# Zero products in 64x32 tiles ahead of the first chain of an attention kernel, and fewer zero products inside it

## Chip, cores and metric

The kernel runs on one core of one Trainium2 chip. The metric is the time of one execution on the device, in microseconds (us); the kernel before takes 241.3 us, the median of three runs (241.25 to 241.42). The profile is of one such execution; its span, first to last instruction, is 239.6 us.

## The reference

An attention with 32 memory slots per head, and behind it a bilinear feed-forward layer. Sizes: 8 batches, 8 heads, 576 positions, head width 64; model width 512, inner width 1536.

```python
def _attn_ref(q, k, v, phi):                 # q, k, v: (8, 8, 576, 64); phi: (8, 8, 576, 32)
    a = softmax(phi over its 32 slots)
    k_m = np.einsum('bhsm,bhsd->bhmd', a, k)
    v_m = np.einsum('bhsm,bhsd->bhmd', a, v)
    scores = 1 / np.sqrt(64) * np.matmul(q, k_m.transpose(0, 1, 3, 2))
    attn = softmax(scores over the slots)
    return np.matmul(attn, v_m)

def _moe_ref(x, w_a, w_b, w_out):            # x: the attention's output, (4608, 512)
    return (x @ w_a * (x @ w_b)) @ w_out
```

## The kernel before

Every instruction is placed by hand: each engine takes its instructions in the order in which the program names them. Batches are handled one after the other in "chains" of short named units. In the first chain, that of batch 0, TensorE has little to do between waits, and the kernel puts products of zeros there ("fill"). Their results are never read.

```python
    warm = consts.tile([P, 512], F16, name="warm")
    nc.vector.memset(warm, 0.0)
    # ... [cut]
    def fill(n, cols=512):
        pw = banks.tile([P, 512], F32, name="pw")
        for _ in range(n):
            nc.tensor.matmul(pw[:, :cols], warm[:, :P], warm[:, :cols], start=True, stop=True)
```

The units of a chain that the reader meets below (b is the batch, g the half of its heads):

```python
        def exp_phi(z):                       # exp0, exp1: ScalarE
            nc.scalar.activation(out=t["exp"][...], in_=phis[b][...], func=AF.Exp)

        def sums(g, x):                       # ks (x = 0) and vs (x = 1): 36 products in 64x32 tiles each
            pk = banks.tile([P, 2 - x, D], F32, name="pk")
            for i in range(NI):               # NI = 9
                for j in range(4):
                    r, hp = head(g, j)
                    nc.tensor.matmul(pk[32 * j:32 * j + 32],
                                     t["exp"][64 * r:64 * r + 64, hp, i, :],
                                     kvs[b][64 * r:64 * r + 64, part, hp, D * i:D * (i + 1)],
                                     start=(i == 0), stop=(i == NI - 1), tile_position=(64 * r, 32 * j))
            # ... [cut] VectorE: kvm = pk times the reciprocal of the softmax's sum

        def transpose(g, x):                  # kt, vt: TensorE transposes kvm, VectorE copies it to kvT
            ...

        def q_transpose(hp):                  # qt0 to qt3: VectorE
            nc.vector.transpose(out=t["qT"][:, hp, :].bitcast(F32), in_=qs[b][:, hp, :].bitcast(F32))

        def scores(gs):                       # s0, s1: 16 products in 32x32 tiles each
            ...

        def exp_scores(g):                    # e0, e1: ScalarE, E = exp(scores)
            ...

        def denominators(g, hfs):             # den00 ...: one product of 128x128 for each half, ScalarE takes its Ln
            for hf in hfs:
                nc.tensor.matmul(pD, ones, t["E"][:, g, sl], start=True, stop=True)
                nc.scalar.activation(out=t["L", g][:, sl], in_=pD, func=AF.Ln)

        def normalise(g, hfs):                # nr00 ...: ScalarE R = exp(-L), VectorE A = E times R
            ...
    # hv, v: "fold", kvT times the weights (pva); hx, x: its copies to vab; a, b: "up" products (pa, pb) of vab and A
```

The program of the chains names them in order. `f18` is `fill(18, 128)`, `L` asks for the loads of a later batch, and `y3` in chain 1 takes three products of the output layer (po).

```python
    def chain(b, plan):
        for x in plan.split():
            if x[0] == "f":
                fill(int(x[1:]), P)
            # ... [cut]
            else:
                us[b][x]()

    fill(64, P)
    chain(0, "exp0 exp1 f18 ks0 ks1 f4 kt0 qt0 qt1 f2 kt1 f4 qt2 qt3 f2 s0 e0 f2 den00 s1 e1 f8 den10 nr00 nr10 vs0 vs1 ...")
    chain(1, "exp0 y3 exp1 y8 ks0 y1 qt0 y2 kt0 y2 qt1 s0 ks1 y3 e0 y1 kt1 qt2 y1 qt3 den0 y3 s1 ...")
```

The loads are asked for by GpSimd in this order: phi, q, v of batch 0 (k comes by two other queues), the weights w_a and w_b in four parts, the output weights and phi, k, q, v of batch 1. Up to eight are under way at a time.

The softmax here doesn't subtract the row's maximum and nothing guards it: scores larger than these inputs give would overflow.

## Time and profile before

| what | before |
|---|---|
| time, median of three | 241.3 us |
| span of the profile | 239.6 us |
| TensorE with a product in flight | 230.6 us (96%) |
| zero products (pw) | 114 of 3092 |
| first and last start of one | 1.3 and 18.3 us |
| DMA traffic from 8 to 30 us | about 205 GB/s |
| share of TensorE in the chain that ended last | 77% |
| share of DMA in it | 16% |

PE is TensorE's products, PEld its weight loads (one for each product), DVE VectorE, ACT ScalarE, POOL GpSimd. Products overlap: a row's first start and its length until the last end say more than the busy time. "Idle before <- X" is the time in which the engine had nothing under way and what ended it; "issue" means that it waited for nothing that the profile shows. The chain that ended last is followed back from the last instruction, at each step to what released it.

### The profile page before, as it was taken

How to read it: one execution, taken by the hardware profiler on the slowest of the kernel's cores; microseconds unless marked ns; L12 is line 12 of the kernel's file. 1: busy time of each engine (PE TensorE's matmuls, PEld its weight loads, DVE VectorE, ACT ScalarE, POOL GpSimd, SP SyncE). 2: the span in 40 equal slices, each digit the busy share in tenths (PEclk: the TensorE clock that was granted, in tenths of full speed). 3: DMA queues.
4: the chain of work that ended last, by engine and by line, in shares of the span. 5: the costliest groups of instructions: out<-in, count | busy, mean ns of one | idle time of the engine just before them, and what ended most of it. 6: DMA issues, size and time to landing. Idle time of an engine off the chain costs nothing.

```text
span 239.6 us, 7764 instructions
## 1 busy us (share of the span) xinstructions
PE 230.6 (96%) x3092; PEld 170.3 (71%) x3092; DVE 165.4 (69%) x403; ACT 158.7 (66%) x410; POOL 159.5 (67%) x135
## 2 busy tenths in 40 slices
PE   7958999999999999999999999999999999999993
PEld 7734664456757867878787787878787778888882
DVE  4636784469949878966975659775976585756642
ACT  2266671669698599687776867797776877465330
POOL 7953244499979629981799948984769087937001
PEclk9999999999999999999999999999999999999998
DMA  6999999999967954992359945599130303032155
GB/s 230 239 197 207 206 258 206 252 213 279 224 154 161 214 115 98 222 208 49 43 123 233 211 90 65 141 212 191 41 85 11 81 16 74 10 83 61 38 130 125
DMA packets 28164, 34.71 MB, mean 145 GB/s; under 512 B 4416, under 2 KB 22208, under 8 KB 28128
## 3 DMA queue, kind: packets, MB, share of 16 engines
q0 software_dynamic: 19264, 23.14, 52.2%
q1 hardware_dynamic: 8352, 10.29, 18.4%
q10 hardware_dynamic: 512, 0.79, 1.0%
q8 instruction: 24, 0.39, 0.7%
q14 instruction: 12, 0.10, 0.1%
HBM read 42.47 MB, written 9.44 MB: 217 GB/s over the span
## 4 chain that ended last, share of the span: by engine, by line
PE 77%; DMA 16%; DVE 2%; issue 1%; POOL 1%; ACT 1%; DVEq 0%; POOLq 0%
PE py L473 18%; PE pa L601 18%; PE pb L601 17%; PE pv L473 9%; DMA wb_sb<-in_moe_w_b_dram 6%; DMA q_sb<-in_q_dram 5%; PE pva L343 5%; DMA kv_sb<-in_v_dram 4%; PE px L473 4%; PE po L398 2%; PE pkv L212 2%; PE pscore L297 1%; PE pD L320 1%; DVE ht L612 1%; ACT a_sb L609 1%
## 5 line engine op out<-in xcount | busy, mean ns | idle before, releaser
L612 DVE TENSOR_TENSOR ht<-a_sb,pb 128x288 f16<-128x288 f16 x168 | 73.3, 450 | 37.5 <-ACT a_sb L609 26.8
L601 PEld LDWEIGHTS <-vab 128*128 128x128 f16 x768 | 72.4, 98 | 24.9 <-issue 7.8
L609 ACT CAST a_sb<-pa 128x288 f16<-128x288 f32 x168 | 66.7, 407 | 25.7 <-PE pa L601 24.6
L601 PE MATMUL pa<-A,vab 128*128 128x288 f16 x384 | 75.8, 287 | 0.1
L601 PE MATMUL pb<-A,vab 128*128 128x288 f16 x384 | 75.0, 286 | 0.7 <-ACT vab L355 0.5
L455 POOL TENSOR_TENSOR h_sums<-ht 128x768 f16<-128x768 f16 x28 | 46.0, 1644 | 33.9 <-DVE ht L612 33.7
L473 PEld LDWEIGHTS <-h_sums 128*128 128x128 f16 x384 | 37.0, 98 | 7.7 <-issue 1.1
L355 DVE CAST vab<-pva 128x512 f16<-128x512 f32 (+1 forms) x52 | 32.3, 644 | 4.8 <-PE pva L343 4.2
L355 ACT CAST vab<-pva 128x512 f16<-128x512 f32 (+1 forms) x52 | 27.7, 569 | 7.8 <-PE pva L343 7.2
L473 PEld LDWEIGHTS <-ht 128*128 128x128 f16 x288 | 28.1, 98 | 5.7 <-issue 0.4
L473 PE MATMUL py<-w_sums,h_sums 128*128 128x256 f16 x192 | 31.3, 273 | 0.0
L455 POOL TENSOR_TENSOR h_sums<-h_sums,ht 128x768 f16<-128x768 f16 x14 | 23.0, 1640 | 1.0
L455 POOL TENSOR_TENSOR h_sums<-ht,h_sums 128x768 f16<-128x768 f16 x14 | 23.0, 1642 | 0.9
L310 ACT ACTIVATE E<-pscore 128x288 f16<-128x288 f32 x32 | 11.4, 419 | 11.4 <-PE pscore L297 11.2
L331 POOL TENSOR_TENSOR A<-E,R 128x576 f16<-128x576 f16 x12 | 15.3, 1278 | 4.3 <-ACT R L329 4.3
L473 PE MATMUL py<-wo_sb,ht 128*128 128x256 f16 x96 | 16.7, 273 | 0.0
L473 PE MATMUL pv<-w_sums,h_sums 128*128 128x256 f16 x96 | 16.5, 273 | 0.0
L473 PE MATMUL py<-w_sums,ht 128*128 128x256 f16 x96 | 15.9, 272 | 0.1
L473 PE MATMUL px<-wo_sb,ht 128*128 128x256 f16 x96 | 15.9, 273 | 0.0
L321 ACT ACTIVATE L<-pD 128x288 f32<-128x288 f32 x32 | 11.5, 418 | 6.0 <-PE pD L320 5.8
L480 ACT ACTIVATE u<-py 128x256 f32<-128x256 f32 x32 | 12.5, 390 | 4.3 <-PE py L473 3.7
L203 DVE STREAM_TRANSPOSE qT<-q_sb 128x288 f32<-128x288 f32 x32 | 14.6, 464 | 0.3 <-DMA q_sb<-in_q_dram 0.3
(65 smaller groups left out, 275.7 us busy)
## 6 DMA issues: line engine op xcount, KB each, us to landing
out_dram<-o_sb SPq DMA_DIRECT2D x68, 128.0 KB, 2.4
phi_sb<-in_phi_dram POOLq DMA_DIRECT2D x8, 576.0 KB, 5.4
kv_sb<-in_v_dram POOLq DMA_DIRECT2D x7, 576.0 KB, 10.3
kv_sb<-in_k_dram POOLq DMA_DIRECT2D x7, 576.0 KB, 6.6
q_sb<-in_q_dram POOLq DMA_DIRECT2D x6, 576.0 KB, 13.1
wo_sb<-in_moe_w_out_dram POOLq DMA_DIRECT2D x6, 256.0 KB, 13.7
q_sb<-in_q_dram POOLq DMA_DIRECT2D x4, 288.0 KB, 9.7
wa_sb<-in_moe_w_a_dram POOLq DMA_DIRECT2D x2, 512.0 KB, 13.8
```

Of the source, the lines that this page charges most:

```text
L203: nc.vector.transpose(out=t["qT"][:, hp, :].bitcast(F32), in_=qs[b][:, hp, :].bitcast(F32))
L310: nc.scalar.activation(out=Ev[:, g, :, z, :], in_=pss, func=AF.Exp, scale=1.0 / (8.0 * CS))
L321: nc.scalar.activation(out=t["L", g][:, sl], in_=pD, func=AF.Ln)
L331: engine.tensor_tensor(out=attn[b][:, g, sl], in0=t["E"][:, g, sl], in1=t["R", g][:, sl], op=ALU.mult)
L343: nc.tensor.matmul(t["pva", lo, z][g][0][32 * j:32 * j + 32, 0:hi - lo], t["kvT"][64 * r:64 * r + 64, 4 + g, M * j:M * j + M], w_sbs[z][64 ...
L355: engine_copy(out=vabs[b][z][:, g, lo:hi], in_=pva[:, 0:hi - lo])
L455: engine.tensor_tensor(out=out, in0=in0, in1=in1, op=op)
L473: nc.tensor.matmul(po, lhs[:, i], rhs[:, i], start=first and i == 0, stop=i == KH - 1, skip_group_check=not first)
L480: nc.scalar.mul(out=x, in_=po, mul=scale)
L601: nc.tensor.matmul(ps, vabs[b][x][:, g, P * i:P * (i + 1)], attn[b][:, g, HALF * hf:HALF * (hf + 1)], start=(g == 0), stop=(g == 1))
L609: nc.scalar.copy(out=a_sbs[b, i, hf], in_=ps)
L612: nc.vector.tensor_tensor(out=ht[:, i, t0:t0 + HALF], in0=a_sbs.pop((b, i, hf)), in1=ps, op=ALU.mult)
```

## The change

A second helper issues zero products in tiles of 64 rows and 32 columns, 64 columns of zeros each, four column positions in turn. 48 of them stand ahead of the first chain between two groups of the products of before: 46, 48 in tiles, 14, in place of 64. Within the chain the group ahead of the first sums goes from 18 to 8 and the one ahead of the first scores from 4 to 2; the groups of 2 ahead of s0 and of den00 and the group of 8 ahead of den10 go; a group of 4 comes in ahead of vs0. In all there are 138 zero products instead of 114, and fewer of them stand between the chain's own units. It serves to keep TensorE supplied with activity ahead of the chain while standing less in the way inside it. What is computed stays the same.

```diff
+    def fill_tiles(n):
+
+        pw = banks.tile([P, 64], F32, name="pw")
+        for x in range(n):
+            j = x % 4
+            nc.tensor.matmul(pw[32 * j:32 * j + 32], warm[0:64, 0:32], warm[0:64, 0:64],
+                             start=True, stop=True, tile_position=(0, 32 * j))
 ...
-    fill(64, P)
-    chain(0, "exp0 exp1 f18 ks0 ks1 f4 kt0 qt0 qt1 f2 kt1 f4 qt2 qt3 f2 s0 e0 f2 den00 s1 e1 f8 den10 nr00 nr10 vs0 vs1 den01 den11 nr01 f4 vt0 vt1 hv0a nr11 hx0a f6 a0.0 ... [the rest as before]")
+    fill(46, P)
+    fill_tiles(48)
+    fill(14, P)
+    chain(0, "exp0 exp1 f8 ks0 ks1 f4 kt0 qt0 qt1 f2 kt1 f2 qt2 qt3 s0 e0 den00 s1 e1 den10 nr00 nr10 f4 vs0 vs1 den01 den11 nr01 f4 vt0 vt1 hv0a nr11 hx0a f6 a0.0 ... [the rest as before]")
```

## The prediction

> **What bounds the kernel now.** I read the page first. TensorE has something in flight nearly all the time, at full granted clock, so zero products can only cost or save where TensorE waits.

> ```profile
> PE 230.6 (96%) x3092; PEld 170.3 (71%) x3092; DVE 165.4 (69%) x403; ACT 158.7 (66%) x410; POOL 159.5 (67%) x135
> ...
> q8 instruction: 24, 0.39, 0.7%
> ```

> The second line matters more than it looks. TensorE ran 3092 products and as many weight loads, 6184 instructions; 24 packets are 258 instructions each, and 0.39 MB over 6184 is 63 bytes. So I read queue 8 as TensorE's own program, arriving during the run in packets of 256 instructions, 128 products.

> Then the timeline of TensorE in the stage that the change touches (start, duration, what, products, and the idle time before them):

> ```profile
> 13.19 0.51 PE L151 MATMUL pw<-warm 128*128 128x128 f16 x6
> 14.71 0.27 PE L151 MATMUL pw<-warm 128*128 128x128 f16 x2 [1.01 <-issue]
> 14.82 0.28 PE L320 MATMUL pD<-E,ones 128*128 128x288 f16 x1
> 15.03 0.78 PE L260 MATMUL pk<-kv_sb,exp_sb 64*32 64x64 f16 x72
> ```

> A zero product waits for no data, yet one group of eight (f8) breaks in two: from the last start at 13.48 to the next at 14.71 are 1.23 us. The rows of the timeline before it add up to 82+72+4+8+2+8+6+16+2+1+16+6 = 223 products and one more weight load. Counting on, the same happens exactly 128 products later, and again after 5x128 more:

> ```profile
> 20.68 1.22 PEld L601 LDWEIGHTS <-vab 128*128 128x128 f16 x11 [0.33 <-issue]
> ...
> 65.87 0.09 PEld L297 LDWEIGHTS <-kvT 32*32 32x32 f16 x1 [0.17 <-issue]
> ```

> In the record of DMA packets the three packets concerned start at 12.29, 18.48 and 63.55 us, and TensorE goes on 2.42, 2.19 and 2.32 us later. So I take these three as waits for instructions: about 1.15 us at 14.7, 0.35 at 20.7, 0.2 at 65.9. Where DMA traffic is light late in the run, packets start when TensorE is some 185 instructions into a block of 256. I therefore place the request at 120 to 170 instructions of each block (an estimate). The first falls at 7.1 to 8.1 us, so under the full load of that time it waited 4 to 5 us.

> Last, the chain of waits in order of time, for the window up to 46 us:

> ```profile
> 3.70 10.74 DMA kv_sb<-in_v_dram
> ...
> 14.72 15.07 DMA wb_sb<-in_moe_w_b_dram
> ...
> 30.08 11.94 DMA q_sb<-in_q_dram
> 42.02 0.02 issue
> 42.04 0.85 DVE qT L203 x2
> ...
> 42.94 0.44 PE pscore L297 x14
> ```

> Up to 42 us it holds no TensorE work. The input loads run back to back at about 205 GB/s, and the scores of batch 1 wait for the last of q. What TensorE gains before 42 us is waiting time there, unless a load also gets faster.

> [...] the zero products start 106.7 ns apart until 6.2 us, 55.7 ns after. [...] 72 tile products of 64 columns take 0.59 us from first start to last (8.2 ns each), and a change of mode costs about 0.2 us between starts (14.82 to 15.03). [...]

> **The change part by part.** *Ahead of the chain.* Before: 82 zero products (64 and f18), 1.26 to 8.19 us; the first sums then start at 8.41, released by ScalarE's exp of phi. After: 46 x 106.7 ns = 4.91 us, to 6.17; a change of mode, 0.2; 48 tile products x 8.2 ns = 0.4; a change back, 0.2; 14+8 = 22 x 55.7 ns = 1.2 us. That ends at 8.2 us. So nothing moves here, but 116 products have passed instead of 82, and the first request for instructions (product 60 to 85) falls into the tiles, at 6.2 to 6.6 instead of 7.1 to 8.1 us: some 1.2 us earlier.

> *Inside.* The groups f4, f2, f2 and f8 become f2, none, none and none; 14 products go. Those around the first scores cost nothing, because the scores wait for the transposed q (DVE until 11.32). f8 is 0.45 us of zero products, 0.33 of them ahead of the stall and inside the 1.01. The new f4 ahead of the v sums costs 0.2 us.

> *Where the first stall goes.* After 223.5 products the program again runs dry. Now 116+72+4+8+2+8+2 = 212 lie ahead of the first scores, so it runs dry at their twelfth of 16 products, at about 11.5 us instead of 13.5. The packet: request at 6.4, wait 3.5 to 5, then 2.3 to 2.4 to TensorE's next product gives 12.3 to 13.8, about 12.9. From there by the durations of before: rest of the scores and exp of E 1.1 us, first denominator, scores of the second half 0.35, their exp until 2.55 us after the stall's end. There the denominator den10 starts: 15.45 against 14.82. From den10 run Ln, two exps and two multiplies to the scaled v (kvm, 16.47, 1.65 us after den10), on which the v transposes and the rest of batch 0 wait. So batch 0 is about 0.6 us late (0 to 1.5).

> *The second stall.* After 24 more products in all, the boundary lies 48 instructions earlier in the work, at the first "up" product (18.6 us, 19.2 with the delay). Its request comes before the first stall now (10.7 against 12.8 us), plus the 8.0 us that the second took gives 18.7. It no longer stalls: minus 0.4 us. Net at 36 us: about 0.2 late. The wait for q at 42 us (vector engine idle 0.26, TensorE 0.42) takes that up.

> *After 42 us.* TensorE is the bound: gaps over 0.12 us between starts add up to only 2.2 us. The seventh stall had 7.6 us from request to boundary and needed 7.3 to 7.6; shifted by 48 instructions it has 9.0, so 0.2 us go. The fifth has 6.75 instead of 8.2 where it needed 6.7, so a small stall could appear.

> Sum: 241.3 + 0.6 - 0.4 - (0.2, hidden by the wait for q) - 0.15 = about 241.2 us.

> **The rivals.** *The stall disappears.* If the early request meets a still short queue and is served within 2.7 us, den10 starts at 14.05 and batch 0 gains up to 0.7 us. For it: the early packets of phi go at 400 GB/s, twice the later rate. Against it: the next two packets waited over 4 us too. Even then the loads of k (landed 36.6, just when TensorE was ready) and q hide the gain: 241.0.

> *The stall in the scores is worse than the one it replaces.* There it delays a chain of exp, denominator, scores and exp, while before two of these had passed. With the packet at 13.8, batch 0 is 1.5 late, 1.1 after the second stall's gain, 0.8 after q's slack: 242.0.

> *The clock.* If tile products do not count as activity or fewer zero products let the clock fall, the 22 products ahead and the first sums run at half rate: about 1.2 us more at 8.2 and perhaps 241.8. Against it: 0.4 us of tiles behind 4.9 us of full products is little, and the page shows full clock through the gap of 1.2 us.

> *A load changes.* Each instruction packet holds one DMA engine for about 0.95 us; of v's shares, 15 had landed by 13.2 us and the last at 14.4. The packets come sooner but not more often before 42 us, so q should land at 42.0 again.

> **Range and chances.** All outcomes lie within 1 us of 241.3, because the change moves waits of about 1 us in front of a load that ends at 42 us whatever TensorE does. I take 241.2, with 240.7 to 242.0 for the uncertain packet. Two per cent would be 4.8 us; nothing here reaches it: 1% faster, 98% within, 1% slower.

> **What would show it.** In the profile after: the sums of batch 0 start at 8.4 us again; the group of eight is gone, and an "issue" gap of 1 to 2 us stands inside the first scores at 11.5 to 13; the first instruction packet starts at 10 to 11.5; no gap at the second boundary near 19; q of batch 1 lands at 42.0 within 0.3; scores of batch 1 near 42.9. It is wrong if the scores of batch 0 run without a gap, if the request is not tied to the count of instructions, or if q lands over 0.5 us away from 42.0.

## The result, and the profile after

The changed kernel takes 257.76 us (median of four runs, 257.09 to 258.16) against 241.28 us (241.16 to 241.42) for the kernel before: a ratio of 1.068 [1.0656, 1.0704]. It is 6.8% slower, far outside the predicted 240.7 to 242.0. The page of its profile (first the busy time of TensorE, then the granted clock in 40 slices, queue 8 and one group of products) shows where to look:

```profile
PE 232.8 (91%) x3116; PEld 170.4 (67%) x3116; DVE 178.7 (70%) x403; ACT 159.1 (62%) x410; POOL 159.3 (62%) x135
...
PEclk9977999965799999999999999999999999999999
...
q8 instruction: 24, 0.39, 0.7%
...
L609 PE MATMUL pa<-A,vab 128*128 128x288 f16 x384 | 77.7, 293 | 13.0 <-DVE vab L363 13.0
```

Three things are new. VectorE is busy for 13.3 us more with the same 403 instructions. One "up" product pa waits 13.0 us for VectorE's vab. The clock has two dips, at about 15 to 22 and 53 to 66 us. Queue 8 still brings 24 packets.

**Batch 0 runs partly at half clock.** The timeline of TensorE after (start, duration, what, products, idle before):

```profile
8.44 1.26 PE L268 MATMUL pk<-kv_sb,exp_sb 64*32 64x128 f16 x72 [0.81 <-ACT exp_sb L202]
...
11.03 1.15 PE L305 MATMUL pscore<-qT,kvT 32*32 32x288 f16 x16
...
14.41 0.28 PE L328 MATMUL pD<-E,ones 128*128 128x288 f16 x1 [0.80 <-ACT E L318]
14.54 0.39 PE L151 MATMUL pw<-warm 128*128 128x128 f16 x4
14.85 0.84 PE L268 MATMUL pk<-kv_sb,exp_sb 64*32 64x64 f16 x72
...
18.74 1.17 PE L609 MATMUL pa<-A,vab 128*128 128x288 f16 x4
```

The first sums start where they did. The sixteen first scores take 1.15 us instead of 0.77, the predicted stall for instructions (0.35 us between two starts, 11.52 to 11.87), smaller than expected. The denominator den10 starts at 14.41, 0.41 us *ahead* of before. Then the gain is lost: four pa products take 1.17 us where before they took 0.66. The two rows in the kernel before:

```profile
11.04 0.77 PE L297 MATMUL pscore<-qT,kvT 32*32 32x288 f16 x16
...
18.59 0.66 PE L601 MATMUL pa<-A,vab 128*128 128x288 f16 x4
```

The stretches of 3.40 us from 11.90 and from 15.30 (stretch, length, busy time of the five engines with counts, granted clock, DMA share and GB/s), in the kernel before:

```profile
11.90:15.30 3.40, 1.82 (x65) 0.96 (x64) 0.33 (x1) 1.89 (x6) 2.03 (x3) 1.00 1.38 198
15.30:18.70 3.40, 2.49 (x90) 1.67 (x74) 2.22 (x9) 2.55 (x8) 1.73 (x4) 1.00 1.43 202
```

and in the changed kernel:

```profile
11.90:15.30 3.40, 1.82 (x86) 1.15 (x86) 0.61 (x2) 2.37 (x7) 2.20 (x3) 1.00 1.38 197
15.30:18.70 3.40, 2.79 (x64) 1.80 (x52) 2.21 (x9) 2.25 (x7) 1.61 (x3) 0.51 1.42 199
```

The changed kernel's clock record says: full clock from 5.10 us, half (0.50) from 15.34 to 22.16. In the records of both kernels the time between two changes of the clock is a whole number of steps of 3.41 us (3, 2, 9, 4 and 55 of them in the changed kernel, 68 in that of before). These steps, counted from the first change, are called the clock's windows below. TensorE has a product in flight for the same 1.82 us of the first stretch in both kernels, but this compares unlike things: only in the changed kernel is the stretch such a window (11.92 to 15.34). In the profile of before, counted from 6.21 us, the windows ran from 9.62 to 13.04 and from 13.04 to 16.45 us; the last section compares window with window. In the changed kernel batch 0 ends 1.3 us late: the first output product po starts at 35.53 instead of 34.23.

**One VectorE operation is held.** VectorE's timeline after shows A of batch 1 (the second half's E times R) and the copy behind it:

```profile
48.11 13.66 DVE L339 TENSOR_TENSOR A<-E,R 128x576 f16<-128x576 f16 x1 [0.37 <-ACT R L337]
61.69 0.74 DVE L363 CAST vab<-pva 128x256 f16<-128x256 f32 x2
```

Before, the same operation took 0.46 us:

```profile
47.37 0.46 DVE L331 TENSOR_TENSOR A<-E,R 128x576 f16<-128x576 f16 x1 [0.36 <-ACT R L329]
```

GpSimd's timeline after, with the first and the last pair of its eight weight subtractions:

```profile
48.70 3.23 POOL L448 TENSOR_TENSOR w_sums<-wo_sb 128x768 f16<-128x768 f16 x2
...
58.24 3.21 POOL L448 TENSOR_TENSOR w_sums<-wo_sb,w_sums 128x768 f16<-128x768 f16 x2
```

They are there before too:

```profile
48.74 3.25 POOL L440 TENSOR_TENSOR w_sums<-wo_sb 128x768 f16<-128x768 f16 x2
```

A then ended at 47.83, 0.91 us ahead of them. Now A starts 0.59 us ahead of the first, and ends at 61.77, just after the last (61.45). In the chain of waits that stretch is:

```profile
47.40 0.69 ACT R L337
...
48.11 13.66 DVE A L339
...
62.16 0.90 PE pa L609 x3
```

Where before the chain had DMA until 42 us and TensorE after it, a single 128x576 product of VectorE now stands on the path. The sum: A is 13.20 us longer and starts 0.74 later, which is 13.9. TensorE starts no product between 48.87 and 62.16 us; the clock falls again, at 52.88, and returns at 66.54. So TensorE works 4.4 us at half speed and loses 2.2. Together 16.1; the spans differ by 15.8.

### The profile page after: what moved, and what is told of

Same layout as the page of the kernel before. It is cut to its first block, busy times and chain, and to the rows that moved or that the text cites. A ratio compares the mean times of both kernels' runs of the same rounds, so it can differ in the third digit from the quotient of the medians.

```text
span 255.4 us, 7812 instructions
## 1 busy us (share of the span) xinstructions
PE 232.8 (91%) x3116; PEld 170.4 (67%) x3116; DVE 178.7 (70%) x403; ACT 159.1 (62%) x410; POOL 159.3 (62%) x135
## 4 chain that ended last, share of the span: by engine, by line
PE 83%; DVE 8%; ACT 4%; DMA 2%; issue 1%; DVEq 0%; POOLq 0%
PE pa L609 19%; PE pb L609 18%; PE py L481 17%; PE pv L481 8%; DVE A L339 5%; PE pva L351 5%; PE px L481 4%; PE po L406 4%; DMA phi_sb<-in_phi_dram 2%; PE pkv L220 2%; PE pscore L305 2%; PE pk L268 2%; PE pD L328 1%; ACT L L329 1%; ACT E L318 1%
## 5 line engine op out<-in xcount | busy, mean ns | idle before, releaser
L609 PEld LDWEIGHTS <-vab 128*128 128x128 f16 x768 | 73.3, 99 | 38.9 <-DVE vab L363 13.7
L609 PE MATMUL pa<-A,vab 128*128 128x288 f16 x384 | 77.7, 293 | 13.0 <-DVE vab L363 13.0
L318 ACT ACTIVATE E<-pscore 128x288 f16<-128x288 f32 x32 | 11.4, 419 | 12.3 <-PE pscore L305 12.2
L339 DVE TENSOR_TENSOR A<-E,R 128x288 f16<-128x288 f16 (+1 forms) x6 | 15.3, 2556 | 4.9 <-ACT R L337 4.8
L339 POOL TENSOR_TENSOR A<-E,R 128x576 f16<-128x576 f16 x12 | 15.3, 1275 | 4.3 <-ACT R L337 4.3
L481 PE MATMUL pv<-w_sums,h_sums 128*128 128x256 f16 x96 | 16.5, 273 | 0.0
## 6 DMA issues: line engine op xcount, KB each, us to landing
q_sb<-in_q_dram POOLq DMA_DIRECT2D x6, 576.0 KB, 13.2
wo_sb<-in_moe_w_out_dram POOLq DMA_DIRECT2D x6, 256.0 KB, 13.7
wa_sb<-in_moe_w_a_dram POOLq DMA_DIRECT2D x2, 512.0 KB, 13.8
```

The lines of the kernel that those rows point to most:

```text
L318: nc.scalar.activation(out=Ev[:, g, :, z, :], in_=pss, func=AF.Exp, scale=1.0 / (8.0 * CS))
L339: engine.tensor_tensor(out=attn[b][:, g, sl], in0=t["E"][:, g, sl], in1=t["R", g][:, sl], op=ALU.mult)
L481: nc.tensor.matmul(po, lhs[:, i], rhs[:, i], start=first and i == 0, stop=i == KH - 1, skip_group_check=not first)
L609: nc.tensor.matmul(ps, vabs[b][x][:, g, P * i:P * (i + 1)], attn[b][:, g, HALF * hf:HALF * (hf + 1)], start=(g == 0), stop=(g == 1))
```

## The experiments

The explanation under test has two links. *Clock:* too little TensorE activity within one of the clock's windows halves the clock, and batch 0 is late. *Cliff:* when A is more than about half a microsecond late, it meets GpSimd's subtractions and is held by all eight. The rivals: that the late start alone costs the time, in proportion, without a cliff; that the tile products ahead of the chain, rather than the trimmed chain, cost the clock; and that half clock, not the held A, is the loss.

The time spent at half clock is read from a run's mean granted clock: 2 x (1 - clock) x time, so 0.986 is 6.8 us, two windows. The windows don't lie at the same times in every run: the full clock came at 5.10 us in the changed kernel's trace and at 6.21 in that of before, though both start with the same 46 zero products, at 1.26 us. Runs of one kernel can fall into two groups, about 242 and about 257 us; the ratios below leave the upper group out where a kernel has both, and its runs are counted in a column of their own. The kernel before ran beside them 55, 38 and 39 times, with medians of 241.40, 241.38 and 241.29.

| kernel | median us (range), runs | ratio | runs over 250 us |
|---|---|---|---|
| after_gate | 242.27 (241.63 to 244.01), 20 | 1.005 [1.0034, 1.0067] | 0 |
| inside_only | 241.62 (241.21 to 257.01), 20 | 1.0009 [1.0002, 1.0016] | 1 |
| front_only | two groups, 20 | 1.0011 [1.0003, 1.002] | 10 |
| late_f14 | 257.34 (256.71 to 257.80), 4 | 1.0659 [1.064, 1.0678] | 4 |
| late_f14_gate | 242.16 (242.00 to 243.05), 19 | 1.0031 [1.0022, 1.0039] | 0 |
| late_f7 | 241.75 (241.52 to 257.54), 12 | 1.0009 [0.9998, 1.002] | 3 |
| late_f14_memset | 242.06, 1 | | 0 |
| after_f8 | 258.02 (257.73 to 258.28), 4 | 1.0679 [1.0656, 1.0702] | 4 |
| wide_gate | 241.74 (241.52 to 242.58), 12 | 1.0009 [0.9997, 1.0022] | 0 |
| before_gate | 241.39 (241.19 to 242.31), 12 | 1.0002 [0.9991, 1.0012] | 0 |
| tiles_wide | 242.21 (241.44 to 242.58), 20 | 1.0032 [1.0024, 1.0041] | 0 |
| dense_gate | 241.61 (241.45 to 241.83), 12 | 1.0009 [1.0001, 1.0018] | 0 |

### The cliff taken away: after_gate

GpSimd first copies one column of A, so that its subtractions wait until A is done. All else is the changed kernel.

```diff
     load(3)
+    gate = consts.tile([P, 1], F16, name="gate")
+    nc.gpsimd.tensor_copy(out=gate, in_=attn[1][:, 1, S - 1:S])
     sum_weights()
```

> The changed kernel, but GpSimd copies one element of A of batch 1 before its eight weight subtractions, so it cannot start them before VectorE has made that A. Theory (two links: the clock falls to half at about 15 us, this makes batch 0 about 1.3 us late, and VectorE's product A of batch 1 then falls behind the start of GpSimd's subtractions and is held for 13.7 us): the clock still falls at about 15 us, A takes about 0.46 us, and the time is 241.5 to 243. Rival (the lost clock itself, early and later on, makes the loss): 250 or more, with the clock falling again after 50 us.

The median is 242.27 us: of the 16.5 us that the change costs, 15.5 are gone with one short GpSimd copy (0.21 us) that sets the order. VectorE's timeline of this kernel:

```profile
48.27 0.46 DVE L339 TENSOR_TENSOR A<-E,R 128x576 f16<-128x576 f16 x1 [0.36 <-ACT R L337]
```

A is even later than in the changed kernel (48.11) and takes its 0.46 us; the subtractions start at 49.02. The half clock is still there (15.12 to 21.94 us in this trace), so lateness alone is not the loss. What it costs by itself can be read from the 20 runs, sorted by their time at half clock: up to 1.9 us of it 241.63 (two runs), 3.4 us 241.82 (one), about 7 us 241.91 to 242.34 (ten), about 10 us 243.51 to 244.01 (seven). Eighteen of 20 runs lost the clock for one window or more. So the clock costs up to some 2.4 us, the cliff the rest.

### The lateness made in another way: late_f14, late_f14_gate, late_f7

The kernel before, with fourteen zero products (0.78 us) in chain 1, ahead of den1, far behind the stage of the clock:

```diff
-    chain(1, "... vs0 e1 vs1 y1 den1 y2 ...")
+    chain(1, "... vs0 e1 vs1 y1 f14 den1 y2 ...")
```

> The kernel before with 14 more zero products in chain 1, ahead of its last denominators (den1), 0.78 us of TensorE that delay A of batch 1 by about 0.75 us and touch neither the clock nor batch 0. Theory: A of batch 1 starts at about 48.1 us, is held until about 61.5 us, and the time is 254 to 258 at full clock until about 53 us. Rival (without the lost clock of batch 0 nothing much happens): 241.3 to 242.2.

It takes 257.34 us. VectorE's timeline:

```profile
48.06 13.69 DVE L331 TENSOR_TENSOR A<-E,R 128x576 f16<-128x576 f16 x1 [0.36 <-ACT R L329]
```

The clock is full until 51.67 us here. Neither tiles nor half clock are needed for the 16 us: 0.78 us of delay at the right place is enough. With the same two lines for the gate as in after_gate added (late_f14_gate):

```diff
+    gate = consts.tile([P, 1], F16, name="gate")
+    nc.gpsimd.tensor_copy(out=gate, in_=attn[1][:, 1, S - 1:S])
```

> The kernel before with 14 more zero products ahead of den1 in chain 1 (which alone made 257.3), and GpSimd copying one element of A of batch 1 before its weight subtractions. Theory (the 16 us come from VectorE's A waiting behind GpSimd's subtractions, not from the delay of 0.78 us): A takes 0.46 us, 241.7 to 242.4, no run over 244. Rival (the delay unbalances the later schedule as well): over 245.

It takes 242.16 us, 0.8 over the kernel before, which is the 0.78 us of zero products. A takes 0.46 us again. The trace is of the slowest of the 19 runs (243.05 us), whose clock was half from 14.79 to 21.62 us, and so it also shows the clock's link by itself. Up to A its program is that of late_f14, whose trace has the full clock there. It starts den10 0.23 us earlier than late_f14 (14.84 against 15.07), yet its first po comes 1.15 us later (35.63 against 34.48) and A 0.93 us later (48.99 against 48.06). So two windows at half clock can make A later than the 0.74 us of the changed kernel, without tiles and without a stall in the scores.

Half as many zero products, without a gate (late_f7):

```diff
+    chain(1, "... vs0 e1 vs1 y1 f7 den1 y2 ...")
```

> Half the delay: 7 zero products ahead of den1, 0.39 us. Theory (a cliff: A is held only if it starts less than about 0.6 us before GpSimd's first subtraction, at 48.7 us in every trace so far): A would start at about 47.75 us, 0.95 us ahead of it, and not be held; most runs 241.5 to 242.1, at most a quarter of them near 257. Rival (the loss grows with the delay): 248 to 251 in all runs.

Nine of 12 runs took 241.52 to 241.86 us, three 256.81 to 257.54; those three are the ones with a mean clock of 0.956 to 0.957, against 0.996 or more. That is some 22 us at half clock: the 13.65 us that follow a held A in the traces, and room for two windows ahead of it. In the trace of one of the nine, VectorE's A is

```profile
47.77 0.46 DVE L331 TENSOR_TENSOR A<-E,R 128x576 f16<-128x576 f16 x1 [0.36 <-ACT R L329]
```

and the first subtraction stands at 48.77. So A is free when it starts 1.00 us ahead of GpSimd and held when it starts 0.61 ahead (late_f14). The rival of a loss in proportion falls: 0.39 us of delay cost 0.3 us (the nine runs have a median of 241.67) or 16, 0.78 us cost 16. It also shows what margin the kernel before has: of its runs, 22 had about 7 us or more at half clock, but only four of these were held, and the other 18 took 241.8 to 242.2 us. So in the kernel before half clock brings the hold only now and then.

### What it is that holds A: late_f14_memset

late_f14, with each GpSimd subtraction replaced by two writes of zeros, about as long together. The weight sums are left out, and with them the sense of the last products; the time still tells whether A is held.

```diff
-                nc.gpsimd.tensor_tensor(out=out[:, sl], in0=in0[:, sl], in1=in1[:, sl], op=ALU.subtract)
+                nc.gpsimd.memset(out[:, sl], 0.0)
+                nc.gpsimd.memset(out[:, sl], 0.0)
```

> The kernel with 14 more zero products ahead of den1 (257.3, A held 13.7 us), where GpSimd fills the weight sums with zeros, twice, in place of subtracting; so the sums of the weights are left out. The fills write but do not read. Theory (A has two inputs in SBUF and is held by GpSimd instructions that read there): A takes about 0.46 us although GpSimd is busy, 241.5 to 242.5. Rival (any long run of GpSimd instructions holds it): A lasts until the fills end.

It took 242.06 us (one run). The timelines of VectorE and GpSimd:

```profile
48.09 0.46 DVE L331 TENSOR_TENSOR A<-E,R 128x576 f16<-128x576 f16 x1 [0.36 <-ACT R L329]
```

```profile
48.66 0.76 POOL L440 MEMSET w_sums<- 128x768 f16 x1
```

The writes fill 48.66 to 60.5 us and A, 0.57 us ahead of them, is not held. So at a lead at which the subtractions hold A (0.59 and 0.61 us), writes don't. By the record A had ended 0.11 us ahead of the first write, so this run does not show the two side by side (at 0.46 us it would have ended 0.15 us ahead of the subtractions in late_f14 too, and there it was held). Nor is every VectorE product held: in the kernel before, sixteen products ht, which take one input from SBUF (a_sb) and one from PSUM (pb), run beside the subtractions at no more than 0.46 us each. A takes both of its inputs from SBUF (E and R), and the subtractions read there (wo_sb, w_sums), which the writes of zeros don't. These runs show the hold with that pair alone; what lies behind it, no run shows. A was held for a whole train of eight instructions (about 12.8 us from first start to last end), not for one: in the traces of the changed kernel, of late_f14 and of front_only it ends 0.32 us after the last of them. Why it was held although by the record it starts up to 0.61 us ahead of the first, no run settles.

### Which half of the change loses the clock: inside_only and front_only

inside_only has the front of before and the trimmed inside:

```diff
-    chain(0, "exp0 exp1 f18 ks0 ks1 f4 kt0 qt0 qt1 f2 kt1 f4 qt2 qt3 f2 s0 e0 f2 den00 s1 e1 f8 den10 nr00 nr10 vs0 ...")
+    chain(0, "exp0 exp1 f18 ks0 ks1 f4 kt0 qt0 qt1 f2 kt1 f2 qt2 qt3 s0 e0 den00 s1 e1 den10 nr00 nr10 f4 vs0 ...")
```

> Only the inner part of the change: 64 zero products and f18 ahead as before, the trimmed groups within the chain. Theory (too little activity of TensorE between 11.9 and 15.3 us makes the clock fall): the clock falls between 13 and 20 us, A of batch 1 takes about 13.7 us, the time is 255 to 259. Rival (the tile products ahead, or the earlier instruction packet, are the cause): 241.0 to 241.6.

A miss in the time: 241.62 us, with one run of 20 at 257.01. The clock did fall, in 14 of 20 runs: in seven for one window, in six for two, and in the long one. In the windows view of its trace:

```profile
11.90:15.30 3.40, 1.93 (x74) 1.22 (x74) 0.37 (x2) 2.54 (x8) 2.03 (x3) 0.77 1.39 197
15.30:18.70 3.40, 2.75 (x77) 1.71 (x56) 2.16 (x9) 1.99 (x6) 1.74 (x4) 0.72 1.42 202
```

the granted means of 0.77 and 0.72 are half clock from 13.76 to 17.18. There is no stall in the scores here and den10 starts at 14.03, 0.79 us earlier than before; the half clock takes that back, and A starts at 47.23, clear of GpSimd. The six runs with two windows took 241.7 to 242.0 us. So the trimmed inside loses the clock but not the 16 us.

front_only is the front of the change (46, 48 tiles, 14, then f8) with the inside of before:

```diff
-    fill(64, P)
-    chain(0, "exp0 exp1 f18 ks0 ... [the inside of before]
+    fill(46, P)
+    fill_tiles(48)
+    fill(14, P)
+    chain(0, "exp0 exp1 f8 ks0 ... [the inside of before]
```

> Only the outer part of the change: 46, 48 in tiles, 14 and f8 ahead, the groups within the chain as before. Theory: the clock stays full until the end, A of batch 1 takes about 0.46 us, the time is 240.8 to 241.6. Rival (the tile products do not count as activity or move the clock's windows): the clock falls between 10 and 20 us and the time is over 250.

Half a miss: ten runs took 241.39 to 242.16 us, ten 256.43 to 259.11. I had expected full clock throughout. The timeline of TensorE in one of the ten long runs:

```profile
11.14 1.15 PE L305 MATMUL pscore<-qT,kvT 32*32 32x288 f16 x16
...
13.60 0.62 PE L151 MATMUL pw<-warm 128*128 128x128 f16 x8
```

The stall is in the scores as in the changed kernel. Its clock is half from 14.51 to 21.34 us, although the eight zero products of f8 are there, and A, 0.36 us ahead of GpSimd, takes 13.44 us. So each half of the change can lose the clock, and inside_only did so only in part of its runs. For front_only the mean clock shows it in six (0.991 in three of the short runs, 0.951 to 0.957 in three of the long ones); in the other seven long runs the half clock behind the held A may hide it, so that the stall alone may have been enough there: that is not shown. Both halves together lost the clock in 18 of 20 runs (after_gate).

### Zero products put back, and the tiles without the stall: after_f8, tiles_wide

after_f8 is the changed kernel with only the group ahead of den10 put back.

```diff
-    chain(0, "... s0 e0 den00 s1 e1 den10 nr00 nr10 f4 vs0 ...")
+    chain(0, "... s0 e0 den00 s1 e1 f8 den10 nr00 nr10 f4 vs0 ...")
```

> The changed kernel with only the group of 8 zero products ahead of den10 put back. Theory (the clock falls for want of activity in one window of 3.4 us, and the 8 products are the largest part of what was taken out of it, 0.45 us): fewer windows at half clock than in the gated changed kernel (18 of 20 runs there, two or three windows each); at least a third of the runs stay at 241.2 to 242. Rival (the outer part alone makes batch 0 late enough): nearly all runs at 256 to 259.

A miss: all four runs took 257.73 to 258.28 us. TensorE's timeline:

```profile
11.04 0.77 PE L305 MATMUL pscore<-qT,kvT 32*32 32x288 f16 x11
12.39 0.31 PE L305 MATMUL pscore<-qT,kvT 32*32 32x288 f16 x5 [0.59 <-issue]
```

The stall inside the scores is 0.87 us from start to start in this run (0.35 in the profiled changed kernel). It moves everything behind it, and the clock falls already at 12.79, for three windows; the eight products come at 14.41, too late. A starts at 49.30 and is held 12.88 us.

tiles_wide is the front of the change, with all other zero products packed into products of up to 512 columns: the same columns, a quarter of the instructions, and no gate.

```diff
+        left = n * cols
+        while left:
+            w = min(left, 512)
+            nc.tensor.matmul(pw[:, :w], warm[:, :P], warm[:, :w], start=True, stop=True)
+            left -= w
 ...
-    fill(64, P)
-    chain(0, "exp0 exp1 f18 ks0 ...
+    fill(46, P)
+    fill_tiles(48)
+    fill(14, P)
+    chain(0, "exp0 exp1 f8 ks0 ...
```

> The outer part of the change (48 tile products between zero products ahead of the chain, inner groups as before), but all other zero products up to 512 columns wide, so that 66 products and not 116 stand ahead of the sums and the first packet boundary does not fall into the scores. No wait of GpSimd for A. Theory (the outer part does harm because its count moves the stall into the scores, which leaves a window with too little activity and makes batch 0 late): at most a fifth of the runs near 257, against half of them with the outer part alone; the others 241.3 to 242. Rival (the tile products themselves do it): half or more near 257.

No run of 20 went over 242.58 us, and in none did the clock fall (means of 0.997 or more). TensorE's timeline:

```profile
10.94 0.78 PE L308 MATMUL pscore<-qT,kvT 32*32 32x288 f16 x16
...
14.23 0.78 PE L271 MATMUL pk<-kv_sb,exp_sb 64*32 64x64 f16 x72
```

The scores run without a stall (0.78 us) and the v sums start 0.8 us earlier than before (15.03). So the tile products do no harm in themselves. That their number of instructions does, through where the stall falls, fits this, but here the stall of the scores is gone, not moved by itself. The 0.8 us are not seen in the time: the median is 0.9 above before. By the trace (of a run of 241.44 us), TensorE then waits 0.67 us for k at 36.57 and 0.30 for q's transpose at 42.78, so the gain is given back there. Why most runs are a further 0.8 us slower stays open.

### Is there a better kernel: before_gate, wide_gate, dense_gate

before_gate is the kernel before with the gate; wide_gate packs its zero products up to 512 columns as well (29 instead of 114); dense_gate also has more of them in the waits of batch 0.

```diff
 # dense_gate, chain 0
-    "... s0 e0 f2 den00 s1 e1 f8 den10 nr00 nr10 vs0 vs1 ... vt0 vt1 hv0a ..."
+    "... s0 e0 f8 den00 s1 e1 f12 den10 nr00 nr10 f8 vs0 vs1 ... vt0 vt1 f12 hv0a ..."
```

> The kernel before with nothing but GpSimd's copy of one element of A of batch 1 ahead of its weight subtractions. Theory: 241.2 to 241.6 in most runs, up to 242.5 where the clock was lost for two windows, and no run near 257, where the kernel before has one in twenty. Rival (those rare runs have another cause): some runs over 250.

> The kernel before with the same columns of zeros, but in products of up to 512 columns in place of 128 (29 zero products instead of 114), and GpSimd waiting for A of batch 1 as above. Theory: the same activity holds the clock; with 85 products less ahead, TensorE reaches the first packet boundary at about 18 us, after its packet has landed, so the stall of 1.2 us at 13.5 us goes; batch 0 is 0.4 to 0.7 us earlier until the loads of k and q of batch 1 at 36.6 and 42.0 us hide it; 240.8 to 241.4, no run over 244. Rival (the stall only moves): a gap with no releaser of about 1 us elsewhere before 20 us and 241.3 to 242.

> Zero products up to 512 columns wide, GpSimd waiting for A, and more zero products where TensorE waits anyway: 8 for 2 units of 128 columns ahead of den00, 12 for 8 ahead of den10, 8 ahead of vs0, 12 ahead of hv0a. In ten traces so far every window of 3.41 us after which the clock fell had under 0.278 of the array's cells in use (columns streamed times the share of the array, over the window), every other one over 0.280. Theory: no run loses the clock before its end, all runs 241.3 to 241.9. Rival (the rule fitted to ten traces does not hold, or the added products delay the chain): some runs still at half clock for 3 us or more, or all over 242.

before_gate: 241.39 us, the gate is free. wide_gate: 241.74 us, a miss of 0.3 us by the upper end. Its TensorE timeline shows the prediction's rival of a stall that disappears, played out:

```profile
14.22 0.28 PE L323 MATMUL pD<-E,ones 128*128 128x288 f16 x1 [0.26 <-ACT E L313]
15.05 0.78 PE L263 MATMUL pk<-kv_sb,exp_sb 64*32 64x64 f16 x72 [0.55 <-DMA kv_sb<-in_v_dram]
...
37.12 0.68 PE L263 MATMUL pk<-kv_sb,exp_sb 64*32 64x128 f16 x36 [0.68 <-DMA kv_sb<-in_k_dram]
```

den10 is 0.6 us earlier than before and no stall stands ahead of it, but then the v sums wait for v and those of batch 1 for k. Nothing is won here, where the loads are the bound. dense_gate kept the full clock in 12 of 12 runs (means of 0.997 or more) and took 241.61 us.

None of them beats the undisturbed time of the kernel before. What the gate does take away is a tail: four of the 132 runs of the kernel before took 257.0 to 258.7 us. None of the 75 runs of the five kernels with a gate did, and 39 of these runs are of after_gate and late_f14_gate, whose kernels without the gate took over 256 us in every run. The 12 runs of before_gate alone would be too few to show it.

## Why the prediction was wrong

**The sums start at 8.4, the packet, the stall, the second boundary.** Right in kind. The sums started at 8.44 us. The first instruction packet started at 9.61 (I had 10 to 11.5, 12.29 before), the stall stood inside the first scores, 0.35 us long where I had 1 to 2, and the second boundary ran without a gap. Mis-sized: den10 came at 14.41 instead of my 15.45, because the packet was there sooner. The full clock came at 5.10 us in this run (6.21 in the profile before), so the tiles began at 5.74 instead of 6.4 us; by the prediction's own count the request then falls at about 5.9 us and waited some 3.7 us, the short end of the predicted 3.5 to 5 (an estimate). The changes of mode took 0.15 and 0.13 us between starts, not 0.2; the 0.21 from 14.82 to 15.03 includes the 288 columns of den10 itself. The zero products therefore ended at 7.6 and not 8.2 us, and the sums came at 8.44 because they wait for ScalarE's exp. Until 15.3 us the changed kernel was ahead. q landed at 41.97 (predicted 42.0).

**"Those around the first scores cost nothing."** In time they did not. But with f2, f2, f2 and f8 taken out, f4 put in ahead of vs0 and the front as before (inside_only), 14 of 20 runs lost the clock for a window or more, against 22 of 132 of the kernel before. The prediction gave the removed products no other role, although their purpose is activity.

**The rival "The clock".** This is the first step that failed. It was set aside with "0.4 us of tiles behind 4.9 us of full products is little, and the page shows full clock through the gap of 1.2 us", and was looked for in the wrong place: in the 22 products and the first sums, at 8 us. It came at 15.34, after the thinned window from 11.92 on, and lasted 6.83 us. The argument from before was weak as well: that a kernel keeps the clock through one gap, at one phase of the window, gives no margin. Twenty-two of its 132 runs in fact had about 7 us or more at half clock, against 17 of 20 of the changed kernel with the gate. The lateness of 1.3 us is also larger than the rival's 0.5.

**"The wait for q takes that up."** Partly. Batch 0 was 1.26 us late when the sums of batch 1 began (38.00 against 36.74). The wait for q, in the second scores, took 0.35 of that, a short wait for v of batch 1 ahead of its sums another 0.16, and 0.74 reached A.

**"All outcomes lie within 1 us of 241.3", "Two per cent would be 4.8 us; nothing here reaches it".** This is the step that cost the 16 us. It assumes that lateness is passed on one to one or hidden. The profile before already held the counter-evidence: A ending at 47.83 us, GpSimd's train starting at 48.74. The prediction follows the chain of waits to 46 us and takes what comes after 42 us as bound by TensorE, so a margin of 0.9 us between two other engines, neither of which waited for the other, was not seen.

## What to carry to other kernels

Beside the waits, look for pairs of operations that don't depend on each other but must not meet: a VectorE product of two SBUF tiles, 0.59 us ahead of a train of eight GpSimd subtractions, took 13.66 us here instead of 0.46, and a one-column copy that orders them costs nothing measurable (241.39 us against 241.29). Zero products inside a chain may not be only filler: here half clock followed on a window with 0.23 of the array in use, and the full clock stayed after one with 0.36. Before any is removed or moved, add up the array's use over every window of that length (3.41 us here), at each phase, and compare it with a kernel that keeps the clock in many runs. When a small change moves the time a lot, repeat it often: one kernel here had ten runs at 242 and ten at 257 us.

## What the runs showed of the hardware

What fits 14 traces is the share of the array in use: columns streamed, each weighted by rows x columns of its tile / 16384, over those that could have been. Zero products of 128 columns start 106.7 ns apart at half clock, which is 1200 columns per us; at twice that, an estimate for the full clock (55.7 ns apart there), a window holds 8192. In the changed kernel from 11.92 to 15.34:

```
2 denominators x 288 + 4 zero products x 128, whole array = 1088
16 scores x 288 x 1/16                                    =  288
63 v-sum products x 64 x 1/8                              =  504
                                              1880 / 8192 = 0.23   (half clock follows)
```

In the kernel before from 13.04 to 16.45: twelve zero products and three denominators on the whole array, 2400, and 72 v-sum products, 576: 2976 / 8192 = 0.36, and the clock stays. With a product at the edge of a window shared between the two windows by its columns, the six windows after which the clock fell in the first 33 us have at most 0.277, and the 88 at full clock after which it stayed at least 0.281. With every product counted whole where it starts, as in the sums above, two of them cross (0.297 in front_only fell, 0.275 in before_gate stayed). So the border at 0.28 is a fit to these windows, good to some 0.02; what it does show is that an idle window isn't needed for the fall, and that weighting small tiles by their area sorts these windows where their busy time does not.

Sliding the window over the traces, the changed kernel falls below 0.28 for windows that end anywhere from 12.6 to 15.8 us, nearly every phase, the kernel before only for 14.2 to 15.4, about a third of the phases. Its profile kept the clock by its phase: a window that ended at 15.30 us would have had 0.26. The runs agree in kind: 18 of 20 of after_gate lost a window or more, 22 of 132 of the kernel before. That is the margin which the prediction didn't have.

**A short instruction can be stretched thirtyfold.** A's 0.46 us became 13.66, and the held operation never shows as a wait: in the profile it is one long busy VectorE instruction, and only its duration gives it away.
